# First weight loads spread over two DMA queues, and one tile transposed by DMA, in a two-layer attention and SwiGLU kernel

## The chip, the cores and the metric

The kernel runs on one core of a Trainium2 chip. The metric is the device time of one execution in microseconds (us); lower is better. Each result is the median of several executions.

## The reference

Two layers over x of 2048 tokens and width 1024, with the same weights in both. Each layer is a dilated local attention (32 heads of 32, eight keys at distances 0, 2, ... 14) and a SwiGLU block (inner width 3584), each on a normalised x and added to x.

```
x = x + _A_ref(_layernorm(x, axis=-1), A_wqkv, A_wo)
x = x + _B_ref(_layernorm(x, axis=-1), B_w1, B_w3, B_w2)
x = x + _A_ref(...)      # the same again
x = x + _B_ref(...)
# _A_ref: qkv = x @ wqkv (1024 x 3072); 8-key softmax; o @ wo
# _B_ref: h = silu(x @ w1) * (x @ w3); h @ w2
```

## The kernel before

Every operation is recorded with an estimated duration; a list scheduler then orders the operations of each engine and emits them. Only the first few microseconds matter here: `q_first`, which makes q for the first 512 tokens (four tiles of 128). To start early it does not wait for full normalisation of tiles 0 and 1. It takes their mean, half of tile 0's sum on VectorE and half on ScalarE, subtracts it, transposes the tile on TensorE and multiplies it by q's weights, row block by row block ("rows" 0 to 7 of 128 input channels, 256 KB each) as they arrive. Tiles 2 and 3 are normalised first, transposed, and multiplied afterwards. Then come k and v.

```
dma(... x_sb[0] left half, queue SP);  dma(... x_sb[0] right half, queue AQ)
dma(256, x_sb[1][:], xin[:, 1, :], ..., queue="AQ")     # AQ: issued by ScalarE; default: by SyncE
rows = q_weights(0, "k", load=False)
for kk in range(4):
    rows[2](kk)                    # q's weight rows 0..3
load_x(0, 2, 4)                    # x tiles 2 and 3
rows[2](4)
rows[2](5)
...
act(0.75, ... ACTF.Copy, accum_out=part[:, 1:2]) ...    # ScalarE's half of tile 0's sum
rows[2](6, 2, queue="AQ", after=[("part", 1)])          # rows 6 and 7, behind that sum
...
for j in range(2, TPC):            # tiles 2 and 3
    stats(j); root(j, j + 1); apply(j)
    transposed(xn[j], ...)         # 8 TensorE transposes, copied out by VectorE and ScalarE
...
# q of tiles 2 and 3: 4 groups of 16 matmuls with 256 columns (both tiles)
...
wslots[1] = q_weights(1, "s")      # k's weights, 2 MB, on SyncE
```

Two facts of the program are needed later; both are in the traces. Its DMAs take their completion semaphores in turn from eight (the trace of before shows eight, with 944 landing records each), and in before the ninth to the fourteenth issue each wait until the load that had the semaphore before has landed: the tenth came at 4.98 us, with row 0 landed at 4.96, and the eleventh, row 4, at 5.71, with row 1 landed at 5.70. And a load on ScalarE's queue is an instruction in ScalarE's own stream (in after, ScalarE's next computation starts at 7.45 us, 0.05 us after such an issue ends).

## Time and profile before

| | before |
|---|---|
| median of 6 runs | 1616.09 us (1615.54 to 1616.23) |
| profiled span | 1614.2 us |
| TensorE (PE) busy | 1601.5 us |
| first q matmul starts | 5.89 us |
| k projection starts | 22.54 us |

This is TensorE's row of the page: busy time, share of the span, instructions.

```profile
PE 1601.5 (99%) x7463; PEld 762.6 (47%) x7610; DVE 1121.5 (69%) x1904; ACT 331.3 (21%) x527; POOL 5.2 (0%) x28
```

The kernel is bound by TensorE, so time can be won only where TensorE stands still or does avoidable work. This is TensorE's timeline at the start (start us, duration us, engine, line, operation, names, shapes, count; in brackets the idle time before it and what ended it; here and below, "..." stands for rows left out). In the names, slot is a weight buffer, bank an accumulator, xn a normalised tile and xnT the same transposed, hT the transposed tiles 0 and 1; PE is TensorE, DVE VectorE, ACT ScalarE, SP SyncE, and ACTq or SPq mark a DMA issue in that engine's stream. L428 are transposes, L509 the q matmuls of tiles 0 and 1, L523 those of tiles 2 and 3, L347 begins with k.

```profile
0.77 4.06 PE L285 MATMUL bank<-const-bfloat16-1.0 128*128 128x512 bf16 x10 [0.77 <-PEq L745]
4.98 0.66 PE L428 MATMUL bank<-ident,xn 128*128 128x128 bf16 x8
5.89 1.05 PE L509 MATMUL bank<-hT,slot 128*128 128x128 bf16 x16 [0.25 <-DVE hT L433]
...
7.42 2.83 PE L509 MATMUL bank<-hT,slot 128*128 128x128 bf16 x40
11.16 2.79 PE L509 MATMUL bank<-hT,slot 128*128 128x256 bf16 x24 [0.91 <-DMA slot<-in_A_wqkv_dram]
13.79 1.06 PE L428 MATMUL bank<-ident,xn 128*128 128x128 bf16 x16
...
15.56 7.15 PE L523 MATMUL bank<-xnT,slot 128*128 128x256 bf16 x64
22.54 5.78 PE L347 MATMUL bank<-xnT,slot 128*128 128x512 bf16 x25
```

The ten matmuls at the top are warm-ups on constants. There is one stall, 0.91 us in front of 11.16 (1.08 us counted from the last start at 9.98 and one matmul's pitch of 0.11). And 16 transposes stand at 13.79. From 22.54 on, matmuls of 512 columns follow each other every 0.216 us to the end.

The stall's cause is in the chain of waits that ended last (start us, duration us, what):

```profile
1.66 4.03 DMA slot<-in_A_wqkv_dram
5.70 0.02 issue
5.71 5.40 DMA slot<-in_A_wqkv_dram
11.11 0.05 issue
11.16 2.79 PE bank L509 x24
```

Row 4 could be issued only at 5.71 us, when row 1 had landed and given its semaphore back; it landed at 11.1. ScalarE's timeline shows its half sum (L453) starting at 3.56, as soon as its half of x had landed:

```profile
0.80 0.88 ACTq L257 DMA_DIRECT2D x<-in_A_x_dram  x2
...
3.56 0.63 ACT L453 ACTIVATE xn<-x 128x512 bf16<-128x512 bf16 x1 [1.34 <-DMA x<-in_A_x_dram]
3.57 0.39 ACTq L257 DMA_DIRECT2D slot<-in_A_wqkv_dram  x1
```

### The profile page before, as it was taken

To read this page: it belongs to the slowest core of one execution; us is meant where nothing else is said; L and a number is where in the kernel's file an instruction comes from. 1 tells how busy PE (TensorE), PEld (TensorE's weight loads), DVE (VectorE), ACT (ScalarE), POOL (GpSimd) and SP (SyncE) were. 2 spreads that over 40 slices of the span, in tenths; PEclk is the share of its full clock that TensorE was granted. 3 is DMA by queue.
4 is the path that set the end of the run, shared out by engine and by line. 5 is a ranking of instruction groups with operands and counts; after the bars stand their busy time and mean duration, and the time that the engine had idled before them with its cause. 6 is when DMAs were issued, how large, how long until landed. Compare 5 with 4: busy or idle time off the path is not lost.

```text
span 1614.2 us, 19079 instructions
## 1 busy us (share of the span) xinstructions
PE 1601.5 (99%) x7463; PEld 762.6 (47%) x7610; DVE 1121.5 (69%) x1904; ACT 331.3 (21%) x527; POOL 5.2 (0%) x28
## 2 busy tenths in 40 slices
PE   9999999999999999999999999999999999999999
PEld 6555544444444444444444444444444444444444
DVE  5898888889889888888898729884288832211211
ACT  5423322021211222113211032110321101101110
POOL 1000000000000000000000000000000000000000
PEclk9999999999999999999999999999999999999999
DMA  9834755395548664758645487365873464454451
GB/s 320 228 100 150 224 170 171 118 225 168 171 136 251 195 190 132 217 167 234 189 136 160 160 243 231 122 173 176 253 221 119 158 181 156 144 176 150 156 165 44
DMA packets 350777, 285.80 MB, mean 177 GB/s; under 512 B 72288, under 2 KB 344928, under 8 KB 350688
## 3 DMA queue, kind: packets, MB, share of 16 engines
q1 hardware_dynamic: 350128, 283.67, 58.2%
q8 instruction: 59, 0.97, 0.2%
q10 hardware_dynamic: 560, 0.92, 0.2%
q14 instruction: 30, 0.25, 0.0%
HBM read 238.94 MB, written 29.36 MB: 166 GB/s over the span
## 4 chain that ended last, share of the span: by engine, by line
PE 99%; DMA 1%; issue 0%; SPq 0%; DVE 0%
PE bank L347 98%; DMA slot<-in_A_wqkv_dram 1%; PE bank L523 0%; PE bank L509 0%; PE bank L428 0%; SPq L261 0%; DVE x L688 0%
## 5 line engine op out<-in xcount | busy, mean ns | idle before, releaser
L347 PE MATMUL bank<-xnT,slot 128*128 128x512 bf16 x4955 | 1088.9, 379 | 5.3
L347 PEld LDWEIGHTS <-slot 128*128 128x128 bf16 x5056 | 518.1, 102 | 573.0
L347 PE MATMUL bank<-slot,hT 128*128 128x512 bf16 (+2 forms) x1812 | 387.3, 372 | 1.9
L658 DVE TENSOR_TENSOR hT<-sg,bank 128x512 bf16<-128x512 bf16 x224 | 153.4, 685 | 213.0 <-PE bank L347 196.3
L265 DVE TENSOR_TENSOR scr<-scr 128x1024 bf16<-128x1024 bf16 (+3 forms) x576 | 292.1, 535 | 2.1
L347 PEld LDWEIGHTS <-hT 128*128 128x128 bf16 x1848 | 178.5, 98 | 208.7
L656 ACT ACTIVATE sg<-bank 128x512 bf16<-128x512 f32 x224 | 133.8, 597 | 653.8 <-PE bank L347 613.6
L265 DVE TENSOR_TENSOR scr<-qT,kT 128x2048 bf16<-128x2048 bf16 x128 | 153.7, 1216 | 71.7 <-DMA kT<-qkv_d 70.1
L405 ACT CAST sgt<-bank 128x512 bf16<-128x512 f32 x184 | 107.9, 586 | 290.9 <-PE bank L347 273.1
L265 DVE TENSOR_TENSOR scr<-pA,vT 128x2048 bf16<-128x2048 bf16 x128 | 152.5, 1216 | 0.4
L688 DVE TENSOR_TENSOR x<-x,bank 128x512 bf16<-128x512 bf16 (+1 forms) x66 | 43.7, 669 | 122.7 <-PE bank L347 122.4
L347 PE MATMUL bank<-wo,oT 128*128 128x512 bf16 x502 | 112.6, 379 | 0.5
L313 DVE BATCH_NORM_STATS2 st<-x 128x6 f32<-128x512 bf16 x124 | 81.5, 679 | 11.5 <-DMA x<-in_A_x_dram 11.0
L347 PEld LDWEIGHTS <-oT 128*128 128x128 bf16 x512 | 50.1, 98 | 60.3
L633 DVE TENSOR_TENSOR x<-x,bank 128x512 bf16<-128x512 bf16 x64 | 43.9, 685 | 36.5 <-PE bank L347 35.0
L320 ACT ACTIVATE sd<-mv,epst 128x4 f32<-128x4 f32 (+1 forms) x17 | 5.1, 299 | 182.4 <-DVE mv L316 181.9
L616 DVE STREAM_TRANSPOSE pA<-pB 128x2048 bf16<-128x2048 bf16 x16 | 37.0, 2310 | 0.4
L593 DVE STREAM_TRANSPOSE pB<-pA 128x2048 bf16<-128x2048 bf16 x16 | 37.0, 2310 | 0.4
L656 ACT ACT_TABLE_LOAD x20 | 25.7, 1283 | 51.3 <-PE bank L347 51.1
L265 DVE TENSOR_TENSOR pA<-scr 128x256 bf16<-128x256 bf16 x128 | 35.3, 282 | 0.3
L327 DVE TENSOR_SCALAR xn<-x,mv,rstd 128x1024 bf16<-128x1024 bf16 x62 | 30.8, 541 | 4.6 <-DMA xnT<-xn 4.5
L265 DVE TENSOR_TENSOR oT<-scr 128x256 bf16<-128x256 bf16 x128 | 33.6, 282 | 0.1
(60 smaller groups left out, 210.0 us busy)
## 6 DMA issues: line engine op xcount, KB each, us to landing
slot<-in_B_w_dram SPq DMA_DIRECT2D x160, 1024.0 KB, 5.8
slot<-in_A_wqkv_dram SPq DMA_DIRECT2D x28, 1024.0 KB, 5.2
qkv_d<-sgt SPq DMA_DIRECT2D x92, 256.0 KB, 3.4
qT<-qkv_d SPq DMA_DIRECT2D x16, 512.0 KB, 5.0
slot<-in_B_w_dram SPq DMA_DIRECT2D x16, 512.0 KB, 5.5
kT<-qkv_d SPq DMA_DIRECT2D x14, 544.0 KB, 6.6
vT<-qkv_d SPq DMA_DIRECT2D x14, 544.0 KB, 5.7
out_dram<-x SPq DMA_DIRECT2D x31, 128.0 KB, 4.2
```

The source lines that it names most:

```text
L265: return lambda _: nc.vector.tensor_tensor(o, a, b, op=op)
L313: dve(0.67, lambda _, hh=hh: nc.vector.bn_stats(st[q][:, j, hh, :], x_sb[n][:, hh * 512:(hh + 1) * 512]), [("x", n, hh)] + list(after), [( ...
L320: act(0.3, lambda _: nc.scalar.activation(sd[q][:, j0:j1], mv[q][:, j0:j1, 1], ACTF.Sqrt, bias=epst[:]), [("mv", q, j) for j in range(j0, ...
L327: dve(0.5, lambda _: nc.vector.tensor_scalar(xn[j][:], x_sb[n][:], mv[q][:, j, 0:1], rstd[q][:, j:j + 1], op0=ALU.subtract, op1=ALU.mult), ...
L347: nc.tensor.matmul(bank[a.bank][:, 0:ncol], lhsT=w, rhs=r, start=first and i == 0, stop=last and i == n - 1)
L405: evac(act, 0.59, lambda _, a=a, i=i, m=m: nc.scalar.copy(sgt[i][:, m % 2, :], bank[a.bank][:]), op, [], [("sgt", i, m % 2)], a)
L593: dve(2.31, lambda _: nc.vector.transpose(psmT[:].rearrange("p c d -> p (c d)"), psm[:].rearrange("p w s -> p (w s)")), allA, ["pB"])
L616: dve(2.31, lambda _: nc.vector.transpose(At[:].rearrange("p w s -> p (w s)"), AeT[:].rearrange("p c d -> p (c d)")), ["pB"], allA)
L633: evac(dve, t1(512), lambda _, xs=xs, a=a: nc.vector.tensor_tensor(xs, xs, bank[a.bank][:], op=ALU.add), op, [("x", n, hh)], [("x", n, hh) ...
L656: evac(act, 0.6, lambda _, i=i, a=ag: nc.scalar.activation(sg[i][:], bank[a.bank][:], ACTF.Silu), og, [], [("sg", i)], ag, table="silu")
L658: evac(dve, t1(512), lambda _, i=i, a=au, f=f: nc.vector.tensor_tensor(hT[:, f, :], sg[i][:], bank[a.bank][:], op=ALU.mult), ou, [("sg", i ...
L688: evac(dve, t1(cn), lambda _, xs=xs, a=a, cn=cn: nc.vector.tensor_tensor(xs, xs, bank[a.bank][:, 0:cn], op=ALU.add), op, [("x", n, hh)], [ ...
```

## The change

Its intent: bring row 4 in earlier by using both queues from the start, take eight transposes off TensorE (tile 3 goes through a DMA transpose, and its q is taken in separate passes of 128 columns so that tile 2 need not wait for it), and move k's weights to ScalarE's queue. The diff also orders the statistics of tiles 2 and 3 behind tile 1's first transposed block and joins two of wo's six loads.

```diff
-        for kk in range(4):
+        for kk in range(2):
             rows[2](kk)
+        for kk in range(2, 5):
+            rows[2](kk, queue="AQ")
         load_x(0, 2, 4)
-        rows[2](4)
         rows[2](5)
+        rows[2](6, 2)
 ...
-        rows[2](6, 2, queue="AQ", after=[("part", 1)])
 ...
-            stats(j)
+            stats(j, [("ce", 1, 0)])
 ...
+            if j == 2:
+                transposed(xn[j], ...)
+            else:
+                dma(256, xnT[b][:, :, j * P:(j + 1) * P], xn[j][:], ..., 0, transpose=True)
 ...
-   4 groups x 16 matmuls of 256 columns (tiles 2 and 3 together)
+   for j in (2, 3): 4 groups x 16 matmuls of 128 columns
 ...
-        wslots[1] = q_weights(1, "s")
+        wslots[1] = q_weights(1, "s", after=[("part", 0)], queue="AQ")
 ...
-        (wo in six loads)
+        (wo in five loads)
```

More of the change, by code (lines that the diff above doesn't have):

```diff
@@ L356, with q_weights @@
     wslots = {}
-    def q_weights(which, split, load=True, after=()):
+    def q_weights(which, split, load=True, after=(), **kw):
         ids = [take_slot(), take_slot()]
@@ L370, in q_weights @@
                 dma(1024, v, wqkv_v[:, 4 * h:4 * h + 4, which * D:(which + 1) * D], after,
-                    [("w", i, k) for k in range(4)], 3)
+                    [("w", i, k) for k in range(4)], 3, **kw)
             else:
@@ L468, in q_first @@
         for j in range(2, TPC):
-            stats(j)
+            stats(j, [("ce", 1, 0)])
             root(j, j + 1)
             apply(j)
-            transposed(xn[j], [("xn", j)] * 2, xnT[b][:, :, j * P:(j + 1) * P],
-                       [("xnT", b, j, k // 4) for k in range(KT)])
+            if j == 2:
+                transposed(xn[j], [("xn", j)] * 2, xnT[b][:, :, j * P:(j + 1) * P],
+                           [("xnT", b, j, k // 4) for k in range(KT)])
+            else:
+                dma(256, xnT[b][:, :, j * P:(j + 1) * P], xn[j][:], [("xn", j)], [("xnT", b, j, h) for h in range(2)],
+                    0, transpose=True)
         for j in range(2):
@@ L516, in q_first, with emit @@
         ops = []
-        for g in range(4):
-            lk = [[q_lhs(wslots[0], kk, m)[0] for kk in range(KT)] for m in (2 * g, 2 * g + 1)]
-            def emit(op, g=g, lk=lk, pa=pa):
-                for m in range(2):
-                    for kk in range(KT):
-                        nc.tensor.matmul(bank[pa[g].bank][:, m * 2 * P:(m + 1) * 2 * P], lhsT=lk[m][kk],
-                                         rhs=xnT[b][:, kk, 2 * P:4 * P], start=(kk == 0 and m == 0),
-                                         stop=(kk == KT - 1), skip_group_check=True)
-            ops.append(pr.add("PE", 16 * 0.1092, emit,
-                              [("w", i, k) for i in wslots[0][0] for k in range(4)] +
-                              [("xnT", b, j, h) for j in (2, 3) for h in range(2)],
-                              [], takes=[pa[g]], lag=0.17))
-        store(pa, ops, 2)
+        for j in (2, 3):
+            for g in range(4):
+                lk = [[q_lhs(wslots[0], kk, m)[0] for kk in range(KT)] for m in (2 * g, 2 * g + 1)]
+                def emit(op, g=g, lk=lk, pa=pa, j=j):
+                    for m in range(2):
+                        t0 = m * 2 * P + (j - 2) * P
+                        for kk in range(KT):
+                            nc.tensor.matmul(bank[pa[g].bank][:, t0:t0 + P], lhsT=lk[m][kk],
+                                             rhs=xnT[b][:, kk, j * P:(j + 1) * P],
+                                             start=(kk == 0 and m == 0 and j == 2), stop=(kk == KT - 1),
+                                             skip_group_check=True)
+                ops.append(pr.add("PE", 16 * 0.0558, emit,
+                                  [("w", i, k) for i in wslots[0][0] for k in range(4)] +
+                                  [("xnT", b, j, h) for h in range(2)], [], takes=[pa[g]], lag=0.17))
+        store(pa, ops[4:], 2)
         for m0 in range(0, KT, 2):
@@ L542, in q_first @@
             q_tile(0, 0, which, wslots[which], b, (key, tile_))
-        for t0, t1_ in ((0, 2), (2, 4), (4, 5), (5, 6), (6, 7), (7, 8)):
+        for t0, t1_ in ((0, 2), (2, 4), (4, 6), (6, 7), (7, 8)):
             dma(256 * (t1_ - t0), wo[:, t0:t1_, :], wo_v[:, t0:t1_, :], [("d", 0, 2, 0, 6)], [("wo", t0)], 3)
@@ L630, in t_stage @@
                 op = mm8(a, [(oT[oh][:, t, j * P:(j + 1) * P], wo[:, t, hh * 512:(hh + 1) * 512]) for t in range(KT)],
-                         True, True, [("oT", oh, t) for t in range(KT)] + [("wo", t) for t in (0, 2, 4, 5, 6, 7)], lane=1)
+                         True, True, [("oT", oh, t) for t in range(KT)] + [("wo", t) for t in (0, 2, 4, 6, 7)], lane=1)
                 xs = x_sb[n][:, hh * 512:(hh + 1) * 512]
```

## The prediction

> **What bounds the kernel.** TensorE. The page gives PE busy 1601.5 us of a 1614.2 us span. The chain of waits that ended last is 98% matmuls of the common helper, and PE's waits list only three: 0.9 us for q's weights, 0.8 us at the start, 0.3 us for a VectorE copy. From 22.5 us to the last store, matmuls of 512 columns follow each other every 0.216 us with no wait named, so nothing that the change does after the first q projection can pay. What can pay is when the k projection begins (22.5 us in the timeline).
>
> **The head before.** First q matmul at 5.89 us; then, start to start in the timeline: 128-column matmuls every 0.0558 us, 256-column ones every 0.1092 us, PE transposes every 0.056 us. PE runs dry once: the last matmul of weight row 3 starts at 9.98, row 4 starts at 11.16, which is 1.08 us later than it could have been. Row 4 was issued on SyncE only at 5.71, and landed at 11.12. The DMA view shows some 390 GB/s from 4 to 14 us, so the loads are limited by bandwidth: what counts is their order[...]. [...]
>
> **What the change does, costed.**
> - Row 4 goes out third after the two x tiles on ScalarE's queue, rows 6 and 7 go last. By shared bandwidth I expect row 4 at 9 to 10 us, the last row at about 12: saves up to 1.08 us, probably 0.8.
> - Eight PE transposes of tile 3 go: -0.45 us of PE.
> - 128 passes of 128 columns for 64 of 256: 128 x 0.0558 - 64 x 0.1092 = +0.15 us, if weight loads (98 ns each) stay hidden as they do in the first pass.
> - Tile 3's DMA transpose: before, such a one landed 4 to 5 us after issue. Issued near 12 it lands near 17, just when the four passes of tile 2 end (about 17.6). Expected stall 0 to 0.5 us.
> - k's weights (2 MB) go out on ScalarE at about 9.5 instead of 6.6 and 7.2; they land near 17 and are needed near 21. No stall expected.
>
> Ideal sum: 1.08 + 0.45 - 0.15 = 1.38 us. Expected 0.9 us after small stalls.
>
> **What would make it wrong.** Semaphores of DMAs are reused in turn by eight (the waits before the 9th to 12th load are of this kind). If row 3 or 4 on ScalarE's queue must wait for an earlier load to land, at 5 to 6 us, ScalarE cannot do its half of x tile 0's sum (3.56 us before), and the first q matmul starts up to 2.5 us late: the kernel would then be about 1 us slower. I give that one chance in three. Stage k could also wait for the three queued DMA transposes.
>
> **Predicted:** 1615.2 us, 8 in 10 between 1614.4 and 1616.8. Faster by over 2%: 0.003; within 2%: 0.994; slower by over 2%: 0.003.
>
> **What would show each step.** The timeline: first 128-column q matmul still at 5.9 us (late if ScalarE was blocked); no 1 us gap before row 4's matmuls; one group of eight transposes at 13 to 14 us instead of sixteen; matmul pitch 0.056 us in the tile passes; the first 512-column matmul near 21.5 us instead of 22.5. After it, the same stretch of about 1591.7 us to the span's end.

## The result, and the profile after

| | before | after |
|---|---|---|
| median of 6 runs | 1616.09 us | 1620.64 us |
| range | 1615.54 to 1616.23 | 1619.27 to 1621.67 |
| profiled span | 1614.2 us | 1618.1 us |
| first q matmul | 5.89 us | 9.98 us |
| k projection | 22.54 us | 26.64 us |
| from there to the span's end | 1591.7 us | 1591.5 us |

The ratio is 1.0028 (95% interval 1.0016 to 1.0041). Ratios here are the mean time of one kernel's runs over that of the other's in the same rounds, so not quite the ratio of the medians quoted. The last row says that in the profiled execution the whole loss happens before 26.64 us. The kernel is slower, clear of the noise, by 4.5 us, which is more than the whole stretch of waiting that the change was to remove.

TensorE's timeline after (the kernel's lines have moved: L514 are the q matmuls of tiles 0 and 1, L530 the passes of tiles 2 and 3):

```profile
0.77 4.42 PE L285 MATMUL bank<-const-bfloat16-1.0 128*128 128x512 bf16 x10 [0.77 <-PEq L752]
8.86 1.03 PE L428 MATMUL bank<-ident,xn 128*128 128x128 bf16 x8 [3.67 <-DVE xn L464]
9.98 1.86 PE L514 MATMUL bank<-hT,slot 128*128 128x128 bf16 x16
...
12.50 5.84 PE L514 MATMUL bank<-hT,slot 128*128 128x128 bf16 x64
18.17 0.61 PE L428 MATMUL bank<-ident,xn 128*128 128x128 bf16 x8
...
19.49 7.31 PE L530 MATMUL bank<-xnT,slot 128*128 128x128 bf16 x128
26.64 1.68 PE L347 MATMUL bank<-xnT,slot 128*128 128x512 bf16 x7
```

The stall for row 4 is gone and only eight transposes stand at 18.17, as intended. But the first transposes start 3.88 us later, after 3.67 us of standing still, and the same 16 matmuls that took 1.05 us now take 1.86. ScalarE's timeline tells why it was late:

```profile
0.80 0.88 ACTq L257 DMA_DIRECT2D x<-in_A_x_dram  x2
1.70 0.45 ACTq L257 DMA_DIRECT2D slot<-in_A_wqkv_dram  x1
...
3.15 4.25 ACTq L257 DMA_DIRECT2D slot<-in_A_wqkv_dram  x2
7.45 0.63 ACT L455 ACTIVATE xn<-x 128x512 bf16<-128x512 bf16 x1 [5.22 <-DMA slot<-in_A_wqkv_dram]
```

The third line merges the issues of rows 3 and 4 and runs from 3.15 to 7.40; the half sum (L455) starts right after it, at 7.45 instead of 3.56. Its data had been there since 3.4. The chain of waits names what ended it:

```profile
1.66 5.38 DMA slot<-in_A_wqkv_dram
7.04 0.02 issue
7.07 0.34 ACTq L257
7.40 0.05 issue
7.45 0.07 ACT xn L455
```

Row 1, issued at 1.66, landed at 7.04; only then could row 4 be issued. The listing of the compiled program shows the same thing without a clock: row 4 (into slot 1) is ahead of the sum and waits for the semaphore of row 1.

```
DMACopy slot0 <- in_A_wqkv 128x1024                       # row 2
DMACopy slot0 <- in_A_wqkv 128x1024 [waits DMAHW0]        # row 3, after x tile 0's left half
DMACopy slot1 <- in_A_wqkv 128x1024 [waits DMAHW2]        # row 4, after row 1
Activation xn3, part <- x0 128x512  [waits DMAHW3]        # the half sum
```

In before, row 4 waited for the very same semaphore, but on SyncE, which computes nothing. The 5.22 us in the brackets of ScalarE's timeline are all of its idle time before the sum; the part that the issue added is the 4.0 us from 3.43, when the sum's data landed, to 7.45.

**Where the 4.1 us up to the k projection came from**, from the start times in the two traces:

| | us |
|---|---|
| first q matmul later (5.89 to 9.98), 3.89 of it by the half sum (3.56 to 7.45) | +4.09 |
| 32 matmuls and transposes after it at a pitch of 0.107 instead of 0.056 us | +1.63 |
| passes of 128 columns (128 x 0.0558 - 64 x 0.1092) | +0.15 |
| stall for row 4 gone | -1.08 |
| eight transposes gone (8 x 0.0558) | -0.45 |
| gap before tile 1's transposes gone | -0.19 |
| sum | +4.15 |
| measured (22.54 to 26.64) | +4.10 |

### The profile page after: what moved, and what is told of

Its sections match the earlier page's. It is cut to its first block, busy times and chain, and to the rows that moved or that the text cites. A ratio compares the mean times of both kernels' runs of the same rounds, so it can differ in the third digit from the quotient of the medians.

```text
span 1618.1 us, 19330 instructions
## 1 busy us (share of the span) xinstructions
PE 1611.0 (100%) x7666; PEld 765.1 (47%) x7666; DVE 1120.5 (69%) x1903; ACT 327.2 (20%) x524; POOL 5.2 (0%) x28
## 4 chain that ended last, share of the span: by engine, by line
PE 99%; DMA 0%; DVE 0%; issue 0%; SPq 0%; ACTq 0%; ACT 0%
PE bank L347 98%; PE bank L514 1%; PE bank L530 0%; DMA slot<-in_A_wqkv_dram 0%; PE bank L428 0%; SPq L261 0%; DVE hT L433 0%; DVE xn L464 0%; ACTq L257 0%; DVE x L695 0%; ACT xn L455 0%; DVE mean L457 0%
```

## The experiments

**Theory A.** A wait for a DMA semaphore stands in ScalarE's stream ahead of a computation that starts the critical chain. In addition, the standstill leaves TensorE at half its pace, or lets it fall back to that. The clock's records (the granted share of full speed over time) show a fall to half in two runs: from 8.07 to 11.48 us in a_row23, after an idle time of 1.49 us, and from 9.28 to 12.70 us in a_warm, after one of 3.04 us. How much idle time is enough was not measured. When TensorE first had the full clock differs: the warm-ups start at 0.77 us in every trace, and apart from after and o_loads (and u_loads, which has no record) the records begin with the full clock between 3.50 us (best_all) and 6.70 us (t_free), in before at 4.33. With it a first q matmul near 6 us shifts by some tenths of a us: the first eight transposes took 0.66 us in before and 1.03 in best_loads, and the first q matmul started at 5.89 and 6.16.
**Rival B.** Loads of two queues share bandwidth, so what is needed first lands later (row 1 landed at 7.04 instead of 5.70 us).
**Rival C.** The loss comes from the other parts: DMA transpose, narrow passes, k's weights on ScalarE's queue.

Eleven kernels ran, in three groups, each with five rounds beside the kernel before. All gave correct results.

| run | what | median us (range) | first q matmul | k projection |
|---|---|---|---|---|
| after | the change | 1620.64 (1619.27 to 1621.67) | 9.98 | 26.64 |
| a_row4late | row 4 behind the half sum | 1616.63 (1615.87 to 1616.93) | 6.11 | 22.34 |
| a_row23 | row 4 waits for row 0 | 1617.86 (1616.83 to 1619.73) | 7.39 | 24.86 |
| u_loads | old first loads, rest of change | 1616.26 (1615.76 to 1617.41) | 6.14 | 22.92 |
| o_loads | before with new first loads | 1619.85 (1619.80 to 1620.74) | 9.07 | 26.53 |
| a_warm | more warm-ups, misplaced | 1622.91 (1622.64 to 1623.78) | 14.06 | 29.50 |
| a_warm2 | more warm-ups | 1618.60 (1618.11 to 1620.89) | 10.08 | 25.17 |
| best_loads | before, rows 4-5 and 6-7 swapped | 1615.15 (1614.84 to 1615.21) | 6.16 | 21.69 |
| best_all | same, with rest of change | 1615.82 (1615.63 to 1616.03) | 6.13 | 22.31 |
| best_v2 | same, half of k's weights later | 1616.43 (1615.77 to 1616.79) | 6.14 | 23.16 |
| best_v3 | same, later still | 1617.97 (1617.34 to 1620.15) | 5.77 | 23.25 |
| t_free | all of k's weights later | 1627.83 (1626.01 to 1628.79) | 6.14 | 23.35, then a wait of 8.1 |

The kernel before had 1615.86, 1615.95 and 1616.11 us in the three groups.

### a_row4late: the same loads and queues, one issue moved

```diff
-        for kk in range(2, 5):
+        for kk in range(2, 4):
             rows[2](kk, queue="AQ")
 ...  (behind ScalarE's half sum)
+        rows[2](4, queue="AQ", after=[("part", 1)])
```

> After, but weight row 4 goes out on ScalarE's queue behind ScalarE's half sum of x tile 0 and not ahead of it; queues and the other loads stay. Theory A (ScalarE stood still at row 4's issue, waiting for row 1 to land, and the first tile's sum waited behind it): first q matmul at 5.9 to 6.3 us instead of 9.98, full clock from 4 us on, time 1615 to 1616.3 us. Rival B (the loads of two queues share bandwidth, so everything needed first lands later): first matmuls still late, since rows and x tiles land as in after; time 1618 us or more. Rival C (k's weights on ScalarE's queue, tile 3's DMA transpose or the 128-column passes cost the time): no change, about 1620.6 us.

ScalarE's and then TensorE's timeline:

```profile
3.40 0.33 ACTq L257 DMA_DIRECT2D slot<-in_A_wqkv_dram  x1
3.78 0.63 ACT L455 ACTIVATE xn<-x 128x512 bf16<-128x512 bf16 x1 [1.56 <-DMA x<-in_A_x_dram]
3.83 0.41 ACTq L257 DMA_DIRECT2D slot<-in_A_wqkv_dram  x1
...
6.11 0.61 PE L515 MATMUL bank<-hT,slot 128*128 128x128 bf16 x8 [0.25 <-DVE hT L433]
7.20 0.62 PE L515 MATMUL bank<-hT,slot 128*128 128x128 bf16 x8 [0.48 <-DMA slot<-in_A_wqkv_dram]
```

One instruction moved, and 4.0 us came back. The sum starts at 3.78 and the first q matmul at 6.11, as theory A wanted; the time, 1616.63 us, is a little over the range that I had given it. (With the new order row 4 also gets another, already free semaphore: its issue at 3.83 us shows no wait.) B is small but real: row 1 landed at 7.16 us here too, and TensorE stood still for it, 0.48 us in the last line. C is out as the main cause.

### a_row23: a smaller dose of the same wait

```diff
-        for kk in range(2, 5):
-            rows[2](kk, queue="AQ")
+        rows[2](2, 2, queue="AQ")      # rows 2 and 3 in one load
+        rows[2](4, queue="AQ")
```

> After with weight rows 2 and 3 in one load, so that row 4's issue on ScalarE waits for row 0's landing (4.7 us in after) instead of row 1's (7.04 us). Theory A: first q matmul at about 7.7 us, time between before and after, 1616.5 to 1618.5 us, depending on whether TensorE falls to the slow pace. Rivals B and C: about 1620.6 us.

With one load fewer ahead of it, row 4 takes the semaphore of row 0, which landed at 4.66 us. The sum started at 5.07, the first q matmul at 7.39, and the time fell in between. Three doses of one wait (none, to 4.66, to 7.04 us) give a first q matmul at 6.11, 7.39 and 9.98 us. Each time it comes 2.3 to 2.5 us after the start of the half sum.

This run's trace also shows the pace of TensorE as the profiler records it. Its busy times and clock by stretch (columns: stretch, length, busy us and count of PE, PEld, DVE, ACT, POOL, then the granted clock, DMA share, GB/s), and below them TensorE's timeline:

```profile
5.00:8.00 3.00, 1.27 (x19) 1.11 (x20) 1.65 (x5) 2.45 (x5) 0.00 (x0) 1.00 0.95 345
8.00:11.40 3.40, 3.40 (x36) 3.27 (x34) 2.26 (x6) 1.83 (x4) 0.00 (x0) 0.51 1.08 345
11.50:14.00 2.50, 2.50 (x31) 2.31 (x30) 2.05 (x8) 1.66 (x6) 0.00 (x0) 1.00 0.72 270
...
6.48 0.66 PE L428 MATMUL bank<-ident,xn 128*128 128x128 bf16 x8 [1.49 <-DVE xn L464]
...
8.47 1.06 PE L428 MATMUL bank<-ident,xn 128*128 128x128 bf16 x8
```

A standstill of 1.49 us before 6.48 was followed, at 8 us, by 3.4 us of half clock (0.51), and the same eight transposes took 1.06 instead of 0.66 us. In the trace of after, the clock's records only begin with a full clock at 13.31 us, and the view by stretches prints 1.00 for what lies before; the matmul pitch of 0.107 us until 13.3 says what it was. The warm-ups of after, too, kept a pitch of 0.43 us, twice the 0.216 us of full pace, to the last one at 4.56 us. So the trace of after shows no fall: TensorE was still at half pace when the warm-ups ran out. That the standstill of 3.67 us kept it there is tested by a_warm2 below.

### u_loads and o_loads: the two halves of the change apart

u_loads is after with the first loads of before; o_loads is before with the new first loads (the first hunk of the diff and the removed line behind the sum).

> After with the first loads of before put back; k's weights on ScalarE's queue, tile 3's DMA transpose and the passes of 128 stay. Theory A: first q matmul at 5.9 us, one gap of about 1.1 us for row 4 as in before; time 1615.3 to 1616.3 us. Rival C: 1619 us or more.

> Before with only the new first loads (alternating queues); tile 3, its passes and k's weights as in before. Theory A: the whole loss is in here: row 4's issue stands on ScalarE until row 1 has landed, at about 7 us, first q matmul near 10 us, TensorE at half its pace for some us after that; time 1619.5 to 1622 us. If the loss needed another part of the change as well: under 1618 us.

Both came out as theory A said. The loads alone cost 3.7 us (1619.85 against 1616.11); the rest alone costs about nothing (1616.26 against 1615.86, interval of the ratio 0.9991 to 1.0016). In o_loads row 1 landed at 6.13 us and the sum started at 6.53 instead of 3.56, with the same half pace (16 matmuls in 1.87 us) until 13.5 us. First TensorE's line of u_loads, then ScalarE's of o_loads:

```profile
6.14 1.05 PE L513 MATMUL bank<-hT,slot 128*128 128x128 bf16 x16 [0.29 <-DVE hT L433]
...
6.53 0.63 ACT L455 ACTIVATE xn<-x 128x512 bf16<-128x512 bf16 x1 [4.31 <-DMA slot<-in_A_wqkv_dram]
```

### a_warm, a_warm2: the half pace apart from the delay

More warm-up matmuls on constants fill TensorE's idle time and change no data.

```diff
-    NWARM = 10                                   # a_warm
+    NWARM = 27                                   #   (the added ones with a duration of 0 for the scheduler)

-  lambda op: nc.tensor.matmul(...)               # a_warm2
+  the tenth warm-up operation emits 13 matmuls instead of 1
```

> After with 17 more warm-up matmuls, which fill TensorE's idle time up to the first transposes and change no data. If the idle time itself made TensorE run at half its pace until 13.3 us (theory A, second part): first q matmul still at about 10 us, all 128-column pitches 0.056 us, time about 1618.6 us (2 us less than after) and a scatter under 0.6 us instead of 2.4. If the slow pace has another cause: 1620.6 us with the scatter as before.

This one failed as a test. The added matmuls needed accumulator banks, and the scheduler put most of them behind the first transposes, so they delayed the work (first q matmul at 14.06 us). The second kernel put them into one operation, ahead of everything:

> After with 12 more warm-up matmuls, all in front of the first transposes (the earlier try at this was scheduled behind them, and is no test). They end by about 8.5 us at the latest, so the first q matmul stays at about 10 us. If TensorE's idle time made it run at half its pace until 13.3 us: all pitches 0.056 us, the k projection begins near 24.7 instead of 26.64 us, time about 1618.7 us and a smaller scatter. If the pace has another cause: about 1620.6 us.

```profile
0.77 7.34 PE L287 MATMUL bank<-const-bfloat16-1.0 128*128 128x512 bf16 x22 [0.77 <-PEq L754]
...
10.08 1.05 PE L516 MATMUL bank<-hT,slot 128*128 128x128 bf16 x16 [0.25 <-DVE hT L435]
...
25.17 1.03 PE L349 MATMUL bank<-xnT,slot 128*128 128x512 bf16 x3
```

The first q matmul is as late as in after, but the 16 matmuls take 1.05 us again, and 2.0 us of the 4.5 are gone (1618.60 us against 1620.64, medians of two groups). Between the two traces the k projection moves by 1.5 us (26.64 to 25.17), which fits the +1.63 in the table above; the other half microsecond is not in these two traces. So in this kernel the half pace comes of leaving TensorE idle (3.67 us before the first transposes in after, 1.06 in a_warm2), and it is 1.5 to 2 us of the loss. The scatter shrank in four runs of five (1618.11 to 1618.60) and not in the fifth (1620.89); its mean granted clock is 0.999, that of the other four 1.000, but where it lost its time was not seen, as only one run has a trace.

### best_loads: the stall for row 4 taken away without a wait on ScalarE

```diff
         load_x(0, 2, 4)
-        rows[2](4)
-        rows[2](5)
+        rows[2](6)
+        rows[2](7)
 ...
-        rows[2](6, 2, queue="AQ", after=[("part", 1)])
+        rows[2](4, 2, queue="AQ", after=[("part", 1)])
```

This is the kernel before with two loads exchanged. The load behind ScalarE's sum was already early (it landed at 9.74 us), but it carried rows 6 and 7, which are wanted last.

> Before with one edit: the load that ScalarE issues behind its half sum carries rows 4 and 5, and rows 6 and 7 go last on SyncE. Theory A with order of landing as what counts: rows 4 and 5 land at about 9.8 us, before they are wanted at 10.1, the gap of 1.08 us goes and nothing else moves: k projection at 21.5 us, time 1615.0 us (0.9 to 1.1 us less than before). Rival (bandwidth alone sets the time, whatever the order): rows 6 and 7 then come late instead, and the time stays at 1616.

```profile
6.16 1.21 PE L509 MATMUL bank<-hT,slot 128*128 128x128 bf16 x16
...
7.65 5.45 PE L509 MATMUL bank<-hT,slot 128*128 128x128 bf16 x64
12.94 1.06 PE L428 MATMUL bank<-ident,xn 128*128 128x128 bf16 x16
...
21.69 4.48 PE L347 MATMUL bank<-xnT,slot 128*128 128x512 bf16 x19
```

Rows 4 and 5 landed at 9.87 us. The 64 matmuls at 7.65 now run without a break, and k starts 0.85 us earlier than in before. All five runs (1614.84 to 1615.21) lie below all nine of the kernel before in the same rounds (1615.43 to 1616.88); the ratio is 0.9994, and its interval (0.9980 to 1.0008) still includes 1. It is 5.5 us under after, clear of the noise; that it is 0.8 us under before is likely, but not shown by the interval.

### best_all, best_v2, best_v3, t_free: what the rest is worth on good loads

best_all is after with the loads of best_loads. The other three move k's weights: in best_v2 the first half goes on SyncE and the second on ScalarE once tile 3 is normalised, in best_v3 the second half follows the issue of tile 3's transpose, in t_free both halves do.

```diff
-        wslots[1] = q_weights(1, "s", after=[("part", 0)], queue="AQ")
+        wslots[1] = q_weights(1, "s", after=[("xn", 3)], queue="AQ")            # best_v2 (second half only)
+        wslots[1] = q_weights(1, "s", after=[("xnT", b, 3, 0)], queue="AQ")     # best_v3 (second half), t_free (both)
```

> The same two loads, with the rest of the change (tile 3 by DMA transpose, passes of 128, k's weights on ScalarE). If the rest is worth its 0.3 us of TensorE: 1614.7 us. If its DMA transpose lands late because k's weights are under way beside it, as the trace of the run with the old first loads suggests (19.30 us, wanted at 19.0): no better than the run without it, 1615 to 1615.6 us.

> As the run before, with k's first half of weights back on SyncE and the second half held on ScalarE until tile 3 is normalised, so that less traffic stands beside tile 3's DMA transpose. If contention is what delays the transpose: it lands by 17 us, no stall, 1614.7 us. Otherwise as the run before.

TensorE's timeline of best_all:

```profile
14.20 3.73 PE L529 MATMUL bank<-xnT,slot 128*128 128x128 bf16 x64
18.74 3.73 PE L529 MATMUL bank<-xnT,slot 128*128 128x128 bf16 x64 [0.81 <-DMA xnT<-xn]
22.31 4.05 PE L347 MATMUL bank<-xnT,slot 128*128 128x512 bf16 x17
```

The rest of the change costs 0.67 us on good loads (1615.82 against 1615.15, ranges apart): the DMA transpose, issued at 13.38, landed at 18.70, and the second half of the passes waited 0.81 us for it. That is more than the 0.45 us of transposes saved. best_v2, meant to give the transpose a freer road, waited 1.6 us and had the higher median (the ranges overlap): its second half of k's weights went out only at 12.17 us and landed at 18.53, still beside the transpose.

> The improved first loads with the rest of the change, but both halves of k's weights held until tile 3's DMA transpose has landed. In all runs so far that transpose landed 0.9 to 1.0 us after the last 1 MB load issued before it, whichever queue had that load. If it really stands behind such loads: it now lands 3 to 4 us after its issue at about 13.4, by 17.3 us, and the second half of the passes waits for nothing; k's weights then land at about 23 us or later and the k projection waits for them; time 1617 us or more. If a DMA transpose takes 5 us by itself: it lands at 18.5 us as before.

> The same with k's first half on SyncE ahead of the transposes (landing at 14.5 us) and only the second half held until tile 3's transpose has landed. If the transpose stands behind loads issued before it: it lands by 17.3 us; the second half lands at about 21 us, just when the k projection wants it; time 1614.6 to 1615.2 us, at best 0.3 us under the version with only the loads mended. If not: 1616 us.

Both failed as tests of what they were for. The edit steers the scheduler's order and is no wait on the chip: the weights went out 0.8 us after the transpose's issue, while it was still under way. What they do show is that the transpose does not merely stand behind loads issued before it: in t_free no transfer was moving between 12 and 14 us (0 GB/s), the load came after the transpose, and the transpose still took 6.2 us. These are the lines of DMA landing for the tiles concerned, first of o_loads (whose two transposes were issued as the weights were ending or after), then of t_free (issued about when k's weights were):

```profile
L259 SPq DMA_TRANSPOSE xnT<-xn x2: 1239/1519/1799, 15.7 to 18.0; - x2
DMA to landing us min/median/max: 3.1/3.1/3.1
...
L259 SPq DMA_TRANSPOSE xnT<-xn x3: 1347/1513/3853, 13.5 to 16.6; - x3
DMA to landing us min/median/max: 5.9/6.2/6.6
```

So a transpose of 256 KB took 3.1 us with little beside it; the first one of every other trace, beside a load of 1 MB, took 4.9 us (before) to 7.1 us (a_row23). Why, was not settled: a kernel in which the load truly waits for the transpose was not run. In t_free the late weights also made the k projection wait 8.1 us.

## Why the prediction was wrong

- **Right:** TensorE bounds the kernel, and nothing after the k projection moved (1591.7 and 1591.5 us).
- **Right in size:** the stall of 1.08 us for row 4 went, the transposes saved 0.45 us, the narrow passes ran at 0.056 us a matmul.
- **Wrong, and decisive:** "The timeline: first 128-column q matmul still at 5.9 us". It came at 9.98. The prediction named the mechanism (ScalarE standing at an issue until an earlier load lands) but gave it one chance in three, and made the expected time out of the good case. The order in which loads take semaphores could not be read from the diff; the trace of before did show row 4 waiting for row 1, and the change moved this wait onto an engine that computes.
- **Wrong in size:** "up to 2.5 us late" was 4.09. I had row 1 landing at 5 to 6 us; with two queues it landed at 7.04 (6.13 in o_loads, 7.78 in a_row23).
- **Missing from the sum:** "about 1 us slower" had no term for TensorE's pace. The half pace cost 1.6 us more in the trace (the table above) and 2.0 us in the medians (a_warm2); the prediction's sums assumed the full pace throughout.
- **Wrong:** "Row 4 at 9 to 10 us". It landed at 11.69 because it was issued at 7.07. About 12 was expected for the last load, and that was right: rows 6 and 7 landed at 11.05 and row 4 last of all.
- **Wrong, but without effect in after:** tile 3's transpose took 5.4 us (17.29 to 22.72). TensorE was so late that it did not wait. On good loads the stall was 0.81 us, over the 0 to 0.5 predicted.

The scatter of after (2.4 us against 0.7 in before) fits the clock: its three slowest runs (1621.13 to 1621.67) have a mean granted clock of 0.998, the other three 0.999 or 1.000. This is a correlation in six runs, not a test.

## What to carry to other kernels

Here a load issued by ScalarE, which also computes, was an instruction in ScalarE's stream, and while its semaphore was not free, the work behind it waited though its data was there: row 4's issue waited for row 1, which landed at 7.04 us, and ScalarE started its half sum 4.0 us after the sum's data had landed (3.43 to 7.45). The second queue moved little more meanwhile: DMA moved 371 GB/s with the old order and 387 with the new between 5 and 7 us. So count the loads ahead of each issue against the semaphores, put computing engines' issues behind their critical work, and change which bytes the early load carries before changing queues: that alone took the 1.08 us stall away and brought the median 0.8 us down, about what the larger change was after (the interval of that ratio still includes 1).
